# Softmax steps of two head groups merged, planner constants set anew, and ten more leading transposes, in an attention and two-MLP kernel on one core

## The chip, the cores and the metric

The kernel runs on one core of a Trainium2 chip. The metric is the device time of one execution in microseconds (us). The engines are TensorE (PE; its weight loads are listed apart as PEld), VectorE (DVE), ScalarE (ACT), GpSimd (POOL) and the queue SP, which issues the DMAs.

## The reference

Four batches of eight heads, 576 positions, head size 64. A softmax of `phi` over 32 memory slots pools the keys and values to 32 rows a head; each query attends to these 32 rows (a second softmax); the result, 2304 tokens by 512, goes through a leaky MLP (512 to 2048 to 512) and then through a bilinear one (512 to 1536, two branches multiplied, back to 512):

```python
a = exp(phi - max(phi));  a = a / (sum(a) + 1e-9)
k_m = einsum('bhsm,bhsd->bhmd', a, k);  v_m = einsum('bhsm,bhsd->bhmd', a, v)
s = (q @ k_m.T) / 8;  attn = exp(s - max(s));  attn = attn / (sum(attn) + 1e-9)
x = attn @ v_m                      # 2304 x 512 after the heads are joined
h = x @ w_in;  x = maximum(0.01 * h, h) @ w_out
out = ((x @ w_a) * (x @ w_b)) @ w_out2
```

The weights come as 64-bit floats and are cut to high and low single-precision parts on the chip; a product is the sum of three passes (high by high, low by high, high by low).

## The kernel before, in words

The attention is folded into the first MLP: the pooled values times `w_in` (`vw`, L704) are the weights that the softmax rows (`ahi`, `alo`) meet in `h` (L757). `h` goes through the leaky step on ACT to `g`; `g` times `w_out` is `y` (L796), summed over four chunks c of the 2048 columns into `acc`. From L1008 on the bilinear MLP runs in two halves s of the tokens with seven-product block schemes (`abx`, `abz`, `aby`, then `o` L1102 and `os` L1217).

The start of the program, for batch b and head group g (four heads each): `phi` is loaded (L520), its maximum (L540) and exponential (L541) taken, the result transposed on PE (`ta` L554, `tz` L557) and copied to `en`; `km` (L571) pools the keys and values from `kv` (L533) and a rest `kvr` (L536); `kvn` (L580) scales, `kvt` (L588) transposes, and copies make `kd` (pooled keys) and `vm` (pooled values). `sc` (L632) then makes the scores of one piece x of the positions (320 or 256 columns) for both row halves i, in two PSUM tiles. For each of these two, on its own: DVE transposes it to `sm` (L654), takes the maximum (L662), subtracts (L663); ACT exponentiates (L664); DVE sums, adds a small constant, takes the reciprocal (L667 to L669), multiplies (L672) and transposes back to `at` (L673); a copy gives `ahi` and a subtraction `alo` (L678). Four `win` tiles of chunk 0 (`raw_win`, `cv_win`, L454 to L478) must be converted before the first `vw`; four `wout` tiles (to L484) before the first `y`.

Nothing in the program fixes the order by hand. `Program.order` is a list planner: every operation has a cost per engine, a due time `late` and the tiles that it needs; at each moment an engine takes the ready operation with the earliest due time for which there is room. Due times are worked backwards (`urgency`): the due time of the earliest reader, less a latency (`LAT` between engines, `LAT_SAME` on one engine, `LAT_DMA` after a load), less the operation's own cost, less its `slack`. The targets at the end of this chain are the times of the main PE operations (`h`, `y`, `ab`, `o`), first guessed from `START`, then for five more rounds taken from the order just made; the shortest of the six orders is emitted. So a `slack` that is larger makes an operation, and all that leads to it, due earlier. `LEAD` is how many main operations may be taken ahead of the first one still open. `PE`, `DVE` and the others run what is emitted in that order, each engine in sequence. A tile takes a named room: `x` is three PSUM banks for `sc`, `vw`, `ta`, `tz`, `km` and `kvt`; `sm` has three rooms of its own; `slot` is the large pool of 28.

The 18 transposes at the very start (`warm`, L424) read only the identity matrix and write a tile that nobody reads.

Of the kernel before, what the change touches and what calls it, by code (L numbers as in the profile page):

```python
# [19 lines left out]
P = 128  # L20
# [14 lines left out]

NSLOT = 28
ROOMS = {
    "slot": [f"s{i}" for i in range(NSLOT)],  # L40
    "big": [f"g{i}" for i in range(8)],
    "five": [f"f{i}" for i in range(8)],
    "t": [f"t{i}" for i in range(5)],
    "sm": [f"m{i}" for i in range(3)],
    "kvn": ["kvn0"],
    "h": ["b0", "b1", "b2"],
    "y": ["b3", "b4"],
# [9 lines left out]
LEAD = 12
SLACK = {'phi0': 0.0, ('kv0', 0): 1.0, ('kv0', 1): 0.0, 'kvr0': 3.0, ('q0', 0): 0.0, ('q0', 1): 0.0, ('win0', 0): 5.37, ('win0', 1): 5.37, ('wout0', 0): 8.13, ('wout0', 1): 8.13, 'win': 4.9, 'wout': 4.64, 'wa': 23.6, 'wb': -0.15, 'wout2': 16.8, ('sc', 0, 0): 6.2, ('sc', 0, 1): 3.3, ('sc', 1, 0): 8.05, ('sc', 1, 1): 6.75, ('sc', 2, 0): 11.99, ('sc', 2, 1): 9.96, ('vw', 0, 0): 19.04, ('vw', 0, 1): 7.99, ('vw', 0, 2): 9.35, ('vw', 1, 0): -0.31, ('vw', 1, 1): 19.18, ('vw', 1, 2): 8.18}
START = 17.4
BIAS = 0.5  # L60
POOL_BIAS = 0.8
LAT, LAT_SAME, LAT_DMA = 0.4, 0.1, 1.0
OVER = {'PE': 0.0, 'ACT': 0.0, 'DVE': 0.0, 'POOL': 0.0, 'DMA': 0.0}
BLOCKED = 0.0
DMA_RATE, DMA_FIRST = 355e3, 0.0
# [40 lines left out]
class Program:  # L106
# [13 lines left out]
    def op(self, eng, cost, fn, r=(), w=(), tiles=(), pos=None, ahead=60.0, keep=0, slack=0.0, soon=False):  # L120
        o = Op()
        port = isinstance(eng, Port)
        o.costs = {e: (c - OVER[e]) * SPARE[e] for e, c in (eng if isinstance(eng, dict) else {eng: cost}).items()}
# [20 lines left out]
        self.ops.append(o)  # L144
        return o
# [188 lines left out]
def tile_mem_attention__leaky_mlp__bilinear_mlp(  # L334
# [283 lines left out]
    def sc_both(b, x):  # L618

        cols = piece(2 * b + x)  # L620
        n = cols.stop - cols.start
        qs = [("q", b, g) if b else ("q", b, g, x) for g in range(2)]
        scs = [("sc", b, i, x) for i in range(2)]
        for k in scs:
            tile_of(k, "x", [n])

        def s_sc(T):
            for g in range(2):
                for j in range(2):
# [8 lines left out]
        for i in range(2):  # L638
            sc_part(b, i, x)

    def sc_part(b, g, x):

        cols = piece(2 * b + x)
        n = cols.stop - cols.start
# [8 lines left out]
        tok = ("sm", b, g, x)
        op("DVE", c_dve(n), lambda T: nc.vector.transpose(T[sm].rearrange("p a m -> p (a m)"), T[sc]), r=[sc], w=[tok], tiles=[sc, sm])  # L654
        mx, sr = (stat((k, g, x, NM), NM) for k in ("mx", "sr"))
        kmx, ksr = ("mx", g, x, NM), ("sr", g, x, NM)
        by = two(n)
# [12 lines left out]

        op("DVE", c_dve(n) + 0.3, s_sum, r=[tok], w=[ksr], tiles=[sm])
        op(by, 0, lambda T, e: engines[e].tensor_tensor(T[sm], T[sm], wide(sr), op=ALU.mult), r=[ksr], w=[tok], tiles=[sm])  # L672
        op("DVE", c_dve(n), lambda T: nc.vector.transpose(T[at], T[sm].rearrange("p a m -> p (a m)")), r=[tok], w=[at], tiles=[sm, at])  # L673
        kh, kl = ("ahi", b, g, x), ("alo", b, g, x)
        op(copy_by(n), 0, lambda T, e: copy(e, T[ahi][:, g, cols], T[at]), r=[at], w=[kh], tiles=[at, ahi])
        op(
            two(n), 0,
            lambda T, e: engines[e].tensor_tensor(T[alo][:, g, cols], T[at], T[ahi][:, g, cols].bitcast(F32), op=ALU.subtract),  # L678
            r=[at, kh], w=[kl], tiles=[at, ahi, alo], slack=SLACK["sc", min(b, 2), x],
        )  # L680
# [678 lines left out]
```

## Time and profile before

| | us |
|---|---|
| median of 3 runs | 800.46 (800.13 to 802.74) |
| profiled execution, own time | 801.54 |
| its span, first to last instruction | 799.8 |
| PE busy | 775.5 (97%) |
| DVE busy | 615.9 (77%) |
| ACT busy | 372.6 (47%) |
| POOL busy | 119.9 (15%) |

The profile is that of one execution. "Busy" is the time in which an engine executed something; the granted clock is TensorE's, as a fraction of 2.4 GHz (0.50 is 1.2 GHz). The 40 slices of the page are 20 us each; a digit is the busy share in tenths.

### The profile page before, as it was taken

Reading aid. Unit: us, or ns where it says so; the run is one execution under the profiler, and the core shown is the slowest. Engines: PE = TensorE matmul, PEld = TensorE weight load, DVE = VectorE, ACT = ScalarE, POOL = GpSimd, SP = SyncE. Lnnn points to the kernel's source line nnn. Section 1 sums busy time; section 2 is a strip of 40 time slices with the busy share of each in tenths; the row PEclk is TensorE's granted clock in tenths of the full one; section 3 lists DMA queues with packets and bytes.
Section 4 is the critical chain, followed back from the end, with each engine's and each line's share of the span. In section 5 each row is a group of like instructions: output and inputs, shape, how many; then the busy total and the mean of one; then the engine's idle time right before and its main releaser. Section 6 shows DMA issues by size and latency. Waiting matters only on the chain. (4 is left out here: it accounts for less than half of the span.)

```text
span 799.8 us, 12802 instructions
## 1 busy us (share of the span) xinstructions
PE 775.5 (97%) x4754; PEld 661.9 (83%) x4754; DVE 615.9 (77%) x1179; ACT 372.6 (47%) x810; POOL 119.9 (15%) x176
## 2 busy tenths in 40 slices
PE   6689999999999999999999999999999999999998
PEld 4367788989898889899988888888888888888886
DVE  5797798689868986676756988998864666798855
ACT  4557676757444754444435635444321154232210
POOL 0132051014003500010000302131210100024100
PEclk6679999999999999999999999999999999999999
DMA  9974211367143722033878854666487988777402
GB/s 331 387 233 143 91 70 54 99 203 246 46 145 111 273 65 79 1 107 109 304 262 306 277 190 167 227 206 212 166 286 287 310 267 286 233 229 239 150 1 105
DMA packets 56558, 149.99 MB, mean 188 GB/s; under 512 B 7216, under 2 KB 22576, under 8 KB 56496
## 3 DMA queue, kind: packets, MB, share of 16 engines
q1 hardware_dynamic: 56496, 149.18, 54.8%
q8 instruction: 37, 0.61, 0.3%
q14 instruction: 25, 0.20, 0.1%
HBM read 103.55 MB, written 45.61 MB: 187 GB/s over the span
## 5 line engine op out<-in xcount | busy, mean ns | idle before, releaser
L796 PE MATMUL y<-g,wout 128*128 128x320 f32 (+1 forms) x1152 | 216.1, 340 | 1.0 <-DVE wout L484 0.8
L796 PEld LDWEIGHTS y<-g,wout 128*128 128x128 f32 x1152 | 187.5, 190 | 23.1 <-issue 6.3
L1008 PE MATMUL abx<-yb_T,wo 128*128 128x512 f32 x432 | 110.2, 390 | 0.0
L1102 PE MATMUL o<-p,wout 128*128 128x512 f32 x384 | 94.9, 390 | 0.0
L1008 PEld LDWEIGHTS abx<-yb_T,wo 128*128 128x128 f32 x432 | 80.2, 188 | 16.1 <-ACT t L1019 0.2
L1019 ACT COPY t<-abx 128x512 f32<-128x512 f32 x72 | 42.1, 585 | 101.9 <-PE abx L1008 101.7
L722 ACT ACTIVATE g<-h 128x320 fp32r<-128x320 f32 (+1 forms) x128 | 52.5, 411 | 70.8 <-PE h L757 66.9
L1102 PEld LDWEIGHTS o<-p,wout 128*128 128x128 f32 x384 | 72.0, 188 | 15.3 <-DVE osum L1115 0.4
L757 PE MATMUL h<-ahi,vwh 128*128 128x320 f32 (+1 forms) x256 | 78.5, 307 | 2.7 <-ACT ahi L405 1.8
L757 PE MATMUL h<-alo,vwh 128*128 128x320 f32 (+1 forms) x256 | 76.6, 299 | 1.3 <-POOL alo L388 1.0
L757 PE MATMUL h<-ahi,vwl 128*128 128x320 f32 (+1 forms) x256 | 76.3, 298 | 0.0
L811 DVE TENSOR_TENSOR acc<-y,acc 128x320 f32<-128x320 f32 (+1 forms) x72 | 40.1, 556 | 36.7 <-PE y L796 36.3
L773 DVE TENSOR_TENSOR g<-t,g 128x256 fp32r<-128x256 f32 (+1 forms) x112 | 52.5, 473 | 17.8 <-ACT t L722 17.0
L757 PEld LDWEIGHTS h<-ahi,vwh 128*128 128x128 f32 x256 | 48.9, 191 | 11.6 <-issue 4.5
L722 ACT ACTIVATE t<-h 128x320 f32<-128x320 f32 (+1 forms) x128 | 52.3, 409 | 0.2
L757 PEld LDWEIGHTS h<-alo,vwh 128*128 128x128 f32 x256 | 49.0, 191 | 2.6 <-POOL alo L388 1.6
L757 PEld LDWEIGHTS h<-ahi,vwl 128*128 128x128 f32 x256 | 49.0, 191 | 0.0
L1016 DVE TENSOR_TENSOR t<-abz,t 128x512 f32<-128x512 f32 x48 | 33.0, 687 | 20.0 <-ACT t L1019 10.9
L1115 DVE TENSOR_TENSOR oacc<-o,oacc 128x512 f32<-128x512 f32 x40 | 27.5, 688 | 14.8 <-PE o L1102 13.9
L405 ACT CAST p<-t 128x512 fp32r<-128x512 f32 x31 | 19.2, 620 | 39.9 <-DVE t L1040 26.1
L1008 PE MATMUL abx<-yb_B,wo 128*128 128x512 f32 x144 | 36.9, 392 | 0.0
L1008 PE MATMUL abz<-yb_B,wo 128*128 128x512 f32 x144 | 36.7, 390 | 0.0
(311 smaller groups left out, 1348.2 us busy)
## 6 DMA issues: line engine op xcount, KB each, us to landing
k_wo<-wo SPq DMA_DIRECT2D x32, 512.0 KB, 5.0
wo<-k_wo SPq DMA_DIRECT2D x32, 512.0 KB, 4.6
raw_wout<-in_w_out_dram SPq DMA_DIRECT2D x24, 512.0 KB, 5.6
raw_win<-in_w_in_dram SPq DMA_DIRECT2D x16, 512.0 KB, 5.5
kv<-in_kv_dram SPq DMA_DIRECT2D x16, 512.0 KB, 10.6
k_yb_T<-yb_T SPq DMA_DIRECT2D x8, 512.0 KB, 7.2
raw_wa<-in_w_a_dram SPq DMA_DIRECT2D x8, 512.0 KB, 4.1
raw_wb<-in_w_b_dram SPq DMA_DIRECT2D x8, 512.0 KB, 4.6
```

The lines of the kernel that those rows point to most:

```text
L405: nc.scalar.copy(dst, src)
L722: nc.scalar.activation(dst, src, AF.Prelu, alpha=0.01)
L757: nc.tensor.matmul(T[o], T[w[u]][:, k, fs], T[a[v]][:, k, cols], start=(k == 0 and i == 0), stop=(k == 1 and i == 2))
L773: lambda T, e: engines[e].tensor_tensor(T[g][:, i, 1, to], T[t], T[g][:, i, 0, to].bitcast(F32), op=ALU.subtract),
L796: nc.tensor.matmul(T[o], w[:, u, es], T[g][:, j, v, :], start=(f == 0 and p == 0), stop=(f == 3 and p == 2))
L811: "DVE", c_dve(m), lambda T: nc.vector.tensor_tensor(T[acc][:, i, :], T[o], T[acc][:, i, :], op=ALU.add),
L1008: nc.tensor.matmul(T[o], T[w][:, which, u, k * P:(k + 1) * P], T[ys[v]][:, k, :], start=first and k == 0 and x == 0, stop=k == 1 and x == ...
L1016: op("DVE", 0.69, lambda T: nc.vector.tensor_tensor(T[to], T[o], T[x], op=ALU.add), r=[o, x], w=[to], tiles=[o, x, to])
L1019: op("ACT", 0.59, lambda T: nc.scalar.copy(T[t], T[X]), r=[X], w=[t], tiles=[X, t])
L1102: nc.tensor.matmul(T[o], T[w][:, u, es], T[g][:, at, v, :], start=(x == 0 and k == 0), stop=(x == 1 and k == 2))
L1115: "DVE", c_dve(size), lambda T: nc.vector.tensor_tensor(T[acc][:, i, :], T[o], T[acc][:, i, :], op=ALU.add),
```

## The change

The two row halves of a piece get one `sm` tile, which now lies in a `slot` room (29 slots; the three `sm` rooms are gone). The first transposes and the last transposes, copies and `alo` stay one per half; maximum, subtraction, exponential, sum, reciprocal and multiplication are done once over both halves. `warm` issues 28 transposes. All planner constants are replaced. Core of the diff:

```diff
-NSLOT = 28
+NSLOT = 29
-    "sm": [f"m{i}" for i in range(3)],
+WARM = 28
-LEAD = 12
+LEAD = 9
-SLACK 'phi0': 0.0, ('kv0', 0): 1.0, ('kv0', 1): 0.0, 'kvr0': 3.0, ('q0', 0): 0.0, ('q0', 1): 0.0
+SLACK 'phi0': -5.09, ('kv0', 0): -2.57, ('kv0', 1): -8.21, 'kvr0': 3.72, ('q0', 0): -0.28, ('q0', 1): 1.39
-SLACK ('win0', 0): 5.37, ('win0', 1): 5.37, ('wout0', 0): 8.13, ('wout0', 1): 8.13, 'win': 4.9, 'wout': 4.64
+SLACK ('win0', 0): 3.41, ('win0', 1): 14.49, ('wout0', 0): 9.56, ('wout0', 1): 8.9, 'win': 2.74, 'wout': 8.15
-SLACK 'wa': 23.6, 'wb': -0.15, 'wout2': 16.8, ('sc', 0, 0): 6.2, ('sc', 0, 1): 3.3, ('sc', 1, 0): 8.05, ('sc', 1, 1): 6.75
+SLACK 'wa': 28.21, 'wb': -6.07, 'wout2': 14.85, ('sc', 0, 0): 10.3, ('sc', 0, 1): 2.94, ('sc', 1, 0): 7.58, ('sc', 1, 1): 4.46
-SLACK ('vw', 0, 0): 19.04, ('vw', 0, 1): 7.99, ('vw', 0, 2): 9.35, ('vw', 1, 0): -0.31
+SLACK ('vw', 0, 0): 17.13, ('vw', 0, 1): 8.31, ('vw', 0, 2): 6.08, ('vw', 1, 0): 5.69
-START = 17.4
+START = 15.74
-LAT, LAT_SAME, LAT_DMA = 0.4, 0.1, 1.0
+LAT, LAT_SAME, LAT_DMA = 0.4, 0.1, 1.75
-OVER = {'PE': 0.0, 'ACT': 0.0, ...}
+OVER = {'PE': 0.0, 'ACT': 0.043, ...}
-        for _ in range(18):
+        for _ in range(WARM):
...
-        tile_of(sm, "sm", [NM, M])
+        tile_of(sm, "slot", [2, NM, M])
+        for i in range(2):
+            op("DVE", c_dve(n), lambda T, i=i: nc.vector.transpose(T[sm][:, i]..., T[scs[i]]), r=[scs[i]], w=[toks[i]], ...)
-        op("DVE", c_dve(n), lambda T: nc.vector.tensor_reduce(mx, T[sm], axis=AX.X, op=ALU.max), r=[tok], w=[kmx], ...)
+        op("DVE", c_dve(2 * n), lambda T: nc.vector.tensor_reduce(mx, rows(T), axis=AX.X, op=ALU.max), r=toks, w=[kmx], ...)
-        op("ACT", c_act(n), lambda T: nc.scalar.activation(T[sm], T[sm], AF.Exp, ...), w=[tok], ...)
+        op("ACT", c_act(2 * n), lambda T: nc.scalar.activation(flat(T), flat(T), AF.Exp, ...), w=toks, ...)
...
+        for g in range(2):
+            op("DVE", c_dve(n), lambda T, g=g, at=at: nc.vector.transpose(T[at], T[sm][:, g]...), r=[toks[g]], w=[at], ...)
```

The planner's name for a load's slack carries the chunk: `('win0', x)` is the half x of `win` of chunk 0, `('kv0', g)` the `kv` of batch 0 and group g. `wa` and `wb` slacks are read by no operation: `weight` returns for these kinds ahead of the two operations that take them.

## Rows read from the trace of the kernel before

**Rows 1.** The page, part 1: busy us, share, instructions of PE; part 2: granted clock by slice.

```profile
PE 775.5 (97%) x4754; PEld 661.9 (83%) x4754; DVE 615.9 (77%) x1179; ACT 372.6 (47%) x810; POOL 119.9 (15%) x176
PEclk6679999999999999999999999999999999999999
```

**Rows 2.** Windows: stretch, its length, busy us by engine (instructions), granted clock, DMA share, GB/s.

```profile
0.00:75.00 75.00, 56.36 (x553) 40.33 (x553) 57.41 (x144) 40.81 (x108) 15.75 (x25) 0.77 0.83 291
75.00:796.00 721.00, 719.11 (x4203) 621.58 (x4201) 557.90 (x1036) 331.80 (x703) 104.16 (x151) 1.00 0.52 177
15.00:30.00 15.00, 11.83 (x126) 5.80 (x118) 8.28 (x27) 6.76 (x20) 0.00 (x0) 0.50 1.04 400
30.00:60.00 30.00, 22.84 (x208) 16.59 (x194) 28.31 (x65) 15.40 (x42) 10.01 (x12) 0.80 0.82 279
```

**Rows 3.** Timeline of all engines, 0 to 60 us: start, us, engine, line, operation.

```profile
2.72 1.04 SPq L454 DMA_DIRECT2D raw_win<-in_w_in_dram  x2
7.01 0.75 DVE L540 TENSOR_REDUCE kst<-phi 128x1 f32<-128x576 f32 x1
12.42 0.42 ACT L405 COPY en<-tz 64x128 f32<-64x128 f32 x2
21.93 0.46 DVE L407 COPY kd<-kvt 64x64 f32<-64x64 f32 x2 [1.25 <-ACT vm L405]
36.76 0.85 ACT L405 CAST ahi<-at 128x320 fp32r<-128x320 f32 x2 [3.03 <-DVE at L673]
48.52 2.63 DVE L484 TENSOR_TENSOR wout<-cv_wout,wout 128x512 fp32r<-128x512 f32 x2
```

**Rows 4.** Timeline of PE alone, 0 to 60 us.

```profile
1.36 3.71 PE L424 MATMUL warm<-ident 128*128 128x128 f32 x18 [1.36 <-POOL ident masks.py:199]
8.71 1.12 PE L554 MATMUL ta<-ident,phi 128*128 128x128 f32 x4 [3.65 <-ACT phi L541]
13.53 2.27 PE L571 MATMUL km<-kv,en 128*32 128x128 f32 x32 [2.17 <-DMA kv<-in_kv_dram]
24.34 1.10 PE L704 MATMUL vw<-cv_win,vm 64*32 64x256 f32 x14 [0.78 <-DVE vwl L714]
25.37 1.11 PE L554 MATMUL ta<-ident,phi 128*128 128x128 f32 x4
29.18 1.47 PE L632 MATMUL sc<-q,kd 64*32 64x320 f32 x16 [0.30 <-ACT en L405]
37.27 0.41 PE L757 MATMUL h<-ahi,vwh 128*128 128x320 f32 x1 [1.85 <-ACT ahi L405]
53.02 1.10 PE L704 MATMUL vw<-cv_win,vm 64*32 64x256 f32 x14 [0.86 <-DVE sm L654]
54.05 6.07 PE L796 MATMUL y<-g,wout 128*128 128x320 f32 x24
63.85 2.00 PE L796 MATMUL y<-g,wout 128*128 128x320 f32 x12
```

**Rows 5.** Windows again: around the clock's first fall and its second.

```profile
7.00:8.00 1.00, 0.00 (x0) 0.00 (x0) 1.00 (x3) 0.58 (x2) 0.00 (x0) 0.97 1.05 389
54.00:59.00 5.00, 5.00 (x25) 4.95 (x19) 4.83 (x12) 3.50 (x10) 1.47 (x2) 0.50 0.06 18
```

**Rows 6.** Groups by form, DVE and ACT: busy us, mean ns of one, idle before.

```profile
L662 DVE TENSOR_REDUCE mx<-sm 128x10 f32<-128x320 f32 x4 | 1.7, 458 | 0.0
L663 DVE TENSOR_TENSOR sm<-sm,mx 128x320 f32<-128x320 f32 x4 | 1.8, 483 | 0.0
L540 DVE TENSOR_REDUCE kst<-phi 128x1 f32<-128x576 f32 x8 | 5.8, 744 | 0.0
L842 DVE TENSOR_TENSOR yt_T<-acc,yt_T 128x640 f32<-128x640 f32 x4 | 3.3, 819 | 0.0
L669 DVE RECIPROCAL sr<-sr 128x10 f32<-128x10 f32 x4 | 0.9, 216 | 0.1
L664 ACT ACTIVATE sm<-sm 128x320 f32<-128x320 f32 x8 | 3.4, 470 | 3.0 <-DVE sm L663 3.0
```

More of the change, by code (lines that the diff above doesn't have):

```diff
@@ L55 @@
 TURN = 0.15
+WARM = 28
 SEVEN = 8
[L57 to L59 removed]
+LEAD = 9
+SLACK = {'phi0': -5.09, ('kv0', 0): -2.57, ('kv0', 1): -8.21, 'kvr0': 3.72, ('q0', 0): -0.28, ('q0', 1): 1.39, ('win0', 0): 3.41, ('win0', 1): 14.49, ('wout0', 0): 9.56, ('wout0', 1): 8.9, 'win': 2.74, 'wout': 8.15, 'wa': 28.21, 'wb': -6.07, 'wout2': 14.85, ('sc', 0, 0): 10.3, ('sc', 0, 1): 2.94, ('sc', 1, 0): 7.58, ('sc', 1, 1): 4.46, ('sc', 2, 0): 12.17, ('sc', 2, 1): 10.7, ('vw', 0, 0): 17.13, ('vw', 0, 1): 8.31, ('vw', 0, 2): 6.08, ('vw', 1, 0): 5.69, ('vw', 1, 1): 20.3, ('vw', 1, 2): 8.21}
+START = 15.74
 BIAS = 0.5
[L61 to L63 removed]
+POOL_BIAS = 0.82
+LAT, LAT_SAME, LAT_DMA = 0.4, 0.1, 1.75
+OVER = {'PE': 0.0, 'ACT': 0.043, 'DVE': 0.0, 'POOL': 0.0, 'DMA': 0.0}
 BLOCKED = 0.0
[L65 removed]
+DMA_RATE = 355000.0
 SPARE = {'PE': 1.0, 'ACT': 1.03, 'DVE': 1.03, 'POOL': 1.03, 'DMA': 1.2}
@@ L422, in warm @@
     def warm(T):
-        for _ in range(18):
+        for _ in range(WARM):
             nc.tensor.transpose(T["warm",], ident, ident)
-    op("PE", 5.0, warm, tiles=[("warm",)], ahead=1e12)
+    op("PE", 0.28 * WARM, warm, tiles=[("warm",)], ahead=1e12)
     src_of = {
@@ L637, in sc_both @@
         op("PE", 4 * n / 2.4e3 + TURN, s_sc, r=[*qs, *(("kd", b % 2, g) for g in range(2))], w=scs, tiles=[*qs, *scs])
[L638 to L644, printed above, removed]
         NM = n // 32
-        sc, sm, at = ("sc", b, g, x), ("sm", b, g, x), ("at", b, g, x)
-        tile_of(sm, "sm", [NM, M])
-        tile_of(at, "t", [n])
-        ahi, alo = ("ahi", b), ("alo", b)
+        sm, ahi, alo = ("sm", b, x), ("ahi", b), ("alo", b)
@@ L651, in sc_part, with flat @@
+        tile_of(sm, "slot", [2, NM, M])
         tile_of(ahi, "big", [2, S], F32R)
         tile_of(alo, "big", [2, S], F32R)
[L653 to L657, printed above, removed]
+        toks = [(sm, i) for i in range(2)]
+        def flat(T):
+            return T[sm].rearrange("p i a m -> p (i a m)")
@@ L659, in wide, with rows @@
+        def rows(T):
+            return T[sm].rearrange("p i a m -> p (i a) m")
+        for i in range(2):
+            op(
+                "DVE", c_dve(n), lambda T, i=i: nc.vector.transpose(T[sm][:, i].rearrange("p a m -> p (a m)"), T[scs[i]]),
+                r=[scs[i]], w=[toks[i]], tiles=[scs[i], sm],
+            )
+        mx, sr = (stat((k, x, NM), 2 * NM) for k in ("mx", "sr"))
+        kmx, ksr = ("mx", x, NM), ("sr", x, NM)
         def wide(t):
-            return t.unsqueeze(2).to_broadcast([P, NM, M])
@@ L662, in sc_part @@
-        op("DVE", c_dve(n), lambda T: nc.vector.tensor_reduce(mx, T[sm], axis=AX.X, op=ALU.max), r=[tok], w=[kmx], tiles=[sm])
-        op(by, 0, lambda T, e: engines[e].tensor_tensor(T[sm], T[sm], wide(mx), op=ALU.subtract), r=[kmx], w=[tok], tiles=[sm])
-        op("ACT", c_act(n), lambda T: nc.scalar.activation(T[sm], T[sm], AF.Exp, scale=1.0 / float(D) ** 0.5), w=[tok], tiles=[sm])
+            return t.unsqueeze(2).to_broadcast([P, 2 * NM, M])
+        op("DVE", c_dve(2 * n), lambda T: nc.vector.tensor_reduce(mx, rows(T), axis=AX.X, op=ALU.max), r=toks, w=[kmx], tiles=[sm])
@@ L666, in s_sum @@
+        op(two(2 * n), 0, lambda T, e: engines[e].tensor_tensor(rows(T), rows(T), wide(mx), op=ALU.subtract), r=[kmx], w=toks, tiles=[sm])
+        op("ACT", c_act(2 * n), lambda T: nc.scalar.activation(flat(T), flat(T), AF.Exp, scale=1.0 / float(D) ** 0.5), w=toks, tiles=[sm])
         def s_sum(T):
-            nc.vector.tensor_reduce(sr, T[sm], axis=AX.X, op=ALU.add)
+            nc.vector.tensor_reduce(sr, rows(T), axis=AX.X, op=ALU.add)
             nc.vector.tensor_scalar_add(sr, sr, EPS)
@@ L669, in s_sum @@
             nc.vector.reciprocal(sr, sr)
[L671 to L680, printed above, removed]
+        op("DVE", c_dve(2 * n) + 0.3, s_sum, r=toks, w=[ksr], tiles=[sm])
+        op(two(2 * n), 0, lambda T, e: engines[e].tensor_tensor(rows(T), rows(T), wide(sr), op=ALU.mult), r=[ksr], w=toks, tiles=[sm])
+        for g in range(2):
+            at = ("at", b, g, x)
+            tile_of(at, "t", [n])
+            op("DVE", c_dve(n), lambda T, g=g, at=at: nc.vector.transpose(T[at], T[sm][:, g].rearrange("p a m -> p (a m)")), r=[toks[g]], w=[at], tiles=[sm, at])
+            kh, kl = ("ahi", b, g, x), ("alo", b, g, x)
+            op(copy_by(n), 0, lambda T, e, g=g, at=at: copy(e, T[ahi][:, g, cols], T[at]), r=[at], w=[kh], tiles=[at, ahi])
+            op(
+                two(n), 0,
+                lambda T, e, g=g, at=at: engines[e].tensor_tensor(T[alo][:, g, cols], T[at], T[ahi][:, g, cols].bitcast(F32), op=ALU.subtract),
+                r=[at, kh], w=[kl], tiles=[at, ahi, alo], slack=SLACK["sc", min(b, 2), x],
+            )
```

## The prediction

> **What bounds the kernel now.** The page comes first: PE is busy 97% of the span, and its clock is low only in the first three slices of 20 us [rows 1]. Cutting the span in two tells where time can still be had: from 75 to 796 us PE is busy 719.1 of 721 us at full clock, whereas the first 75 us hold 18.6 us without PE work and a mean clock of 0.77 [rows 2]. So behind 75 us PE itself is the bound and 1.9 us is all that a better order could give there, while a worse one can take any amount; the gain has to come from the start. That leaves two questions for the timelines: what keeps the first `h` until 37.27 us, and what keeps PE from running through between there and 60 us [rows 4].
>
> For the first, the chain runs phi, `ta`, `km`, `kvt`, `kd`, `sc`, softmax, `ahi`, `h`. `kd` is finished at 22.39 us [rows 3], yet `sc` starts at 29.18: PE does the second half of `vw` (24.34) and the transposes of batch 1 (25.37) ahead of it [rows 4]. This is order, not data. For the second, DVE is busy 28.3 of 30 us between 30 and 60 us, where between 15 and 30 it had only 8.3 of 15 [rows 2]: a DVE-bound stretch behind a half idle one.
>
> **The change, part by part.**
>
> *`sc` moves up.* Due times can be worked out from the code; T is the target of the first `h`. Before, back from T over `alo`, `ahi`, transpose, multiplication, sum, exponential, subtraction, maximum, transpose and `sc`, with latencies of 0.1 or 0.4 and slack 6.2, `sc` is due at T-14.4. The two halves of `vw` are due at T-21.7 and T-19.9 (slack 19.04, the second for an `h` 1.76 later). So both `vw` go first, as the timeline shows. After, slack 10.3 and the doubled costs put `sc` at T-20.1, and slack 17.13 puts `vw` at T-19.7 and T-17.9. `sc` is now the most urgent, and I take it to start behind one half of `vw`, at 24.3 instead of 29.18: 4.9 us. Both ends: 6.8 us if it starts when `kd` is there (22.4), 0 if PSUM rooms or the greedy choice leave it where it is.
>
> *The loads change places.* The same arithmetic before gives `win` half 0 at T-33.8, phi T-32.1, `win` half 1 T-32.0, `kvr` T-30.8, `kv` T-29.7, and SP issues in just that order, `win` half 1 third at 2.72 us [rows 3], which is why I trust it. After: `win` half 1 T-39.8 (slack 14.49), `kvr` T-30.8, `win` half 0 T-30.6, phi T-26.2 (slack -5.09), `kv` of group 0 T-25.3, `q` T-22.7, `kv` of group 1 T-19.7. So phi comes behind 1.05 MB of `win` and 0.26 MB of `kvr` that it preceded; at the 389 GB/s of that time [rows 5] that is 3.4 us. `kv` of group 0 has the same bytes ahead of it as before. `en` was complete at 12.84 us and `km` waited for `kv` until 13.53 [rows 3, 4], so 0.7 us of the delay is covered and `km` comes 2.7 us later. Ends: 0 (ACT and DVE free of the interleaved conversions catch up) and 3.4. I take 2.7. It falls on the same chain as the gain of `sc`: the first `h` comes 4.9 - 2.7 = 2.2 us earlier.
>
> *The merged softmax.* Per piece of 320, the four operations over 320 columns that become one of 640 are maximum, subtraction, sum and multiplication: eight of 0.46 to 0.48 us become four. A DVE operation with two inputs takes 0.819 us at 640 columns; a maximum over 576 columns takes 0.744, and by its slope one over 640 some 0.82 [rows 6]. That saves 2x0.458-0.82 = 0.10 twice and 2x0.483-0.819 = 0.15 twice, plus one reciprocal (0.22 [rows 6]) and one addition that I put at the same: 0.94 us of DVE. Three pieces lie ahead of 60 us, so 2.8 us of DVE work go; with DVE 94% busy from 30 to 60, PE gets about 2.5 of them. Ends: 2.8, and 0 if what held PE there were PSUM rooms (the `vw` at 53.02 waited for the DVE transpose of `sm`). The later five pieces save 4.7 us of DVE under a full PE: nothing.
> The merged chain itself is not shorter. Before, `sc` ended at 30.65 and `ahi` began at 36.76, 6.1 us. After: two transposes 0.92, maximum 0.82, subtraction 0.82, exponential some 0.8 (between 0.47, its time at 320 [rows 6], and twice that), sum and its two small ones 1.25, multiplication 0.82, transpose 0.46, two hops between engines 0.2: 6.1. What is lost is that ACT worked on one half while DVE did the other; DVE has an idle 0.9 us during the exponential, into which a `wout` conversion fits.
>
> *Ten more transposes.* 18 take 3.71 us, so 28 end at 1.36 + 5.8 = 7.1 us instead of 5.07. PE was idle until 8.71 anyway [rows 4], and with phi later until some 12.1; nothing waits behind them. What they could give is clock. It stayed at 1.00 until close to 8 us, 2.9 us after the last transpose, and was 0.50 until 31 [rows 2, 5]. The same 2.9 us from 7.1 on end at 10, ahead of `ta` at 12.1: nothing. If phi is not delayed, `ta` and `tz` run at full clock until the wait for `kv`, worth 1 us at most.
> The Trainium skill (TensorE: Matmul & The Clock Gate, Part 4: PE-mode transpose) says that transposes don't count as PE activity for the clock; if so even that 1 us is gone. The trace can't decide it: the clock was full from the first instruction and fell after the transposes had ended.
>
> *The rest.* The slacks of `wa` and `wb` are read by nobody, so these edits are nothing. A slot more, fewer rooms for `sm`, `LEAD` 9, `win` 2.74, `wout` 8.15, `wout2` 14.85 reorder work under a full PE: 0, covered by 163 us of idle DVE from 75 us on [rows 2]; if the cover fails, each late weight costs its conversion, about 0.7 us.
>
> *Sum.* 2.2 + 2.5 = 4.7 us off 801.54, the profiled execution's own time (span 799.8 and 1.7 around it): 796.8. The median of the runs is 1.1 below that execution, so 795.8 for a median.
>
> **The rivals.**
>
> *Full clock (A).* From 54 to 59 us PE works at 0.50 [rows 5] because it had paused at 52 to 53: 24 `y` matmuls take 6.07 us where 12 at full clock take 2.00 [rows 4], so 2.1 us. If the denser order closes this pause, and `sc` starts at 22.4, the sum is 4.7 + 2.1 + 1.9 = 8.7: 791.8. For it: merged tiles free the PSUM rooms of `sc` in two consecutive transposes. Against: DVE remains full, so the pause is likely to move rather than to close.
>
> *Absorbed (B).* The first `h` comes earlier, but `y` waits for `wout`, whose low parts end on DVE at 51.15 us [rows 3], and DVE does the same work up to there less 1.9 us (two pieces), while the phi delay costs DVE the same idle time in front: 800 within 2. For: DVE at 94%. Against: 6.7 us of idle DVE from 15 to 30, which an earlier `sc` fills.
>
> *Slower (C).* phi is late and `sc` doesn't move. The place is `en` at 12.84 against `kv` at 13.53: once `en` comes later than `kv`, each us is one on the whole chain. Then 2.7 us later for `h`, nothing back from DVE, and 1.5 us of stalls in the order made anew behind 75 us, where only loss is possible: 801.54 + 4.2 - 1.1 = 804.6. For: the due times; PE has no slack later to win it back. Against: the same due times move `sc`.
>
> *The change does not do what it says:* the planner emits the best of six rounds by its own length; if its costs place the softmax on DVE in the same gaps, order and time stay as they are. This ends with B at 800.
>
> **How the numbers follow.** The forecast, 793.5 to 798, has 0.45; A 0.16; B with the unchanged order 0.17; C 0.22. The range leaves out the far ends of A (below 789.5) and C (above 803.5): 789.5 to 803.5; the forecast's own range is 793.5 to 798. A measurement of this kernel tells 0.3%, 2.4 us, from no change. Faster by more than that, below 798.1: forecast and A, 0.61; within: B, 0.17; slower, above 802.9: C, 0.22.
>
> **What would show it.** `sc` at 24 to 27 us and the first `h` near 35 show the first step right; `ta` near 12 and `km` near 16 the second. DVE busy between 30 and 60 with about 1 us less per softmax piece, the maximum over 640 columns at 0.82, show the third. The clock at 0.50 from 10 us on shows the transposes idle; a clock of 1.00 at 13 us would make me wrong there. Waits of PE behind 75 us above 3 us in all would show the loss of C. The prediction is wrong if the first `h` does not move earlier and the time falls all the same, or if the time from 75 us on changes by more than the start.

## The result, and the profile after

The changed kernel takes 791.78 us (median of four runs, 790.38 to 792.52) against 800.30 us for the kernel before on the same chip (four runs, 799.77 to 802.74): ratio 0.9886, 95% interval 0.9861 to 0.9911. The forecast was 795.8: right in direction and inside the range, but the gain is 8.5 us where 4.7 were forecast. The profiled execution took 792.19 us, against 801.54 before.

The page of the changed kernel, parts 1 and 2, as in [rows 1]:

```profile
PE 769.7 (97%) x4764; PEld 660.3 (84%) x4764; DVE 604.3 (76%) x1120; ACT 376.4 (48%) x811; POOL 131.6 (17%) x190
PEclk8699999999999999999999999999999999999999
```

PE still has 97%; it is busy 5.8 us less in all, and the low digits of the clock are two instead of three. The same windows as [rows 2]:

```profile
0.00:75.00 75.00, 59.60 (x615) 45.38 (x616) 56.59 (x132) 47.48 (x123) 13.85 (x24) 0.86 0.84 291
75.00:786.00 711.00, 709.63 (x4150) 614.85 (x4149) 547.02 (x988) 328.92 (x688) 117.71 (x166) 1.00 0.53 179
15.00:30.00 15.00, 10.00 (x145) 5.08 (x143) 9.79 (x22) 9.86 (x26) 4.51 (x7) 0.84 1.03 407
30.00:60.00 30.00, 26.97 (x287) 21.03 (x273) 26.72 (x66) 18.46 (x52) 6.51 (x10) 0.82 0.94 321
```

Behind 75 us there is 1.4 us without PE work now, 1.9 before: nothing came from there. In the first 75 us PE does 59.6 us of work at a mean clock of 0.86, where it did 56.4 at 0.77. DVE is busier from 15 to 30 us (9.8 against 8.3) and less busy from 30 to 60 (26.7 against 28.3). PE's timeline, to be laid beside [rows 4]:

```profile
1.36 5.71 PE L424 MATMUL warm<-ident 128*128 128x128 f32 x28 [1.36 <-POOL ident masks.py:199]
13.08 1.12 PE L554 MATMUL ta<-ident,phi 128*128 128x128 f32 x4 [6.01 <-ACT phi L541]
15.41 1.65 PE L571 MATMUL km<-kv,en 128*32 128x128 f32 x32
...
21.03 1.78 PE L632 MATMUL sc<-q,kd 64*32 64x320 f32 x16
...
34.25 0.65 PE L571 MATMUL km<-kvr,en 64*32 64x128 f32 x8 [1.83 <-DMA kvr<-in_kv_rest_dram]
34.83 1.94 PE L571 MATMUL km<-kv,en 128*32 128x128 f32 x32
...
37.28 0.63 PE L760 MATMUL h<-ahi,vwh 128*128 128x320 f32 x1
...
46.28 2.03 PE L799 MATMUL y<-g,wout 128*128 128x320 f32 x12
48.23 0.66 PE L707 MATMUL vw<-cv_win,vm 64*32 64x256 f32 x16
48.83 5.55 PE L799 MATMUL y<-g,wout 128*128 128x320 f32 x36
```

`sc` starts 8.2 us earlier than before (21.03 against 29.18) and yet the first `h` starts at the same time (37.28 against 37.27). The gain comes behind it: 36 `y` follow each other in 5.55 us, where before 12 `y`, a pause, and 24 `y` at half clock stood.

To see where, the matmuls of `h` and `y` (and of the later stages) are numbered from the first `h`, number 0; number 24 is the first `y`, number 36 the thirteenth. Their starts, changed kernel minus kernel before: number 0, 0.0; 24, -1.8; 36, -5.2; 60, -7.5; 144, -9.1 (73.01 against 82.12 us); 600, -9.0; the last one, -9.4. So 5.2 us come between the first `h` and the thirteenth `y`, 2.3 in the next 24 matmuls, 1.6 from there to number 144, and 0.3 in the remaining 713 us.

In the kernel before, PE is idle for 3.9 us between the first `h` and the thirteenth `y`, and in the changed kernel for 1.2. The later waits of the kernel before are for DVE: `y` waits for low parts of the first `wout` weights (L484), and the `vw` at 53.02, right ahead of the thirteenth `y` [rows 4], for a transpose of `sm` that DVE does behind the last of these parts. This last part ended at 51.15 us before [rows 3] and ends at 45.88 now, 5.3 us earlier; in the changed kernel PE waits for nothing between 44.75 us and the thirteenth `y`. The transpose of the kernel before, and the last low part of the changed one:

```profile
52.57 0.40 DVE L654 STREAM_TRANSPOSE sm<-sc 128x256 f32<-128x256 f32 x1
```

```profile
45.20 0.68 DVE L484 TENSOR_TENSOR wout<-cv_wout,wout 128x512 fp32r<-128x512 f32 x1
```

Windows from 15 us up to the end of the last low part, the kernel before and then the changed one:

```profile
15.00:51.15 36.15, 26.73 (x277) 15.90 (x269) 28.11 (x67) 17.64 (x48) 8.55 (x10) 0.72 1.03 376
```

```profile
15.00:45.88 30.88, 22.85 (x282) 14.24 (x283) 23.38 (x53) 18.32 (x49) 11.02 (x16) 0.75 1.04 374
```

DVE's idle time is nearly the same (8.0 and 7.5 us). It is the busy time that fell, from 28.1 to 23.4 us, by 4.7. The groups of DVE from the start up to those two ends, each instruction counted whole, with the mean ns of one behind the comma:

```profile
L475 DVE SCALAR_TENSOR_TENSOR cv_wout<-raw_wout,cv_wout 128x512 int32<-128x512 int32 x4 | 3.8, 1017 | 0.0
L484 DVE TENSOR_TENSOR wout<-cv_wout,wout 128x512 fp32r<-128x512 f32 x3 | 3.3, 1131 | 0.0
L475 DVE SCALAR_TENSOR_TENSOR cv_win<-raw_win,cv_win 128x512 int32<-128x512 int32 x4 | 2.7, 687 | 0.0
L663 DVE TENSOR_TENSOR sm<-sm,mx 128x320 f32<-128x320 f32 (+1 forms) x4 | 2.4, 638 | 0.0
```

```profile
L475 DVE SCALAR_TENSOR_TENSOR cv_wout<-raw_wout,cv_wout 128x512 int32<-128x512 int32 x4 | 2.6, 670 | 0.0
L484 DVE TENSOR_TENSOR wout<-cv_wout,wout 128x512 fp32r<-128x512 f32 x3 | 2.3, 776 | 0.3 <-ACT wout L405 0.3
L663 DVE TENSOR_TENSOR sm<-sm,mx 128x640 f32<-128x640 f32 (+1 forms) x2 | 1.5, 749 | 0.0
```

The four joins L475 on `cv_wout` took 1017 ns each before, though the same operation on `cv_win` took 687: 670 now. The three L484 took 1131 and take 776. These are not other operations, they ran beside other work. The kernel before's joins and its second pair of subtractions in DVE's timeline, and POOL's timeline around them:

```profile
37.34 3.84 DVE L475 SCALAR_TENSOR_TENSOR cv_wout<-raw_wout,cv_wout 128x512 int32<-128x512 int32 x4
47.09 1.51 DVE L663 TENSOR_TENSOR sm<-sm,mx 128x256 f32<-128x256 f32 x2
```

```profile
37.30 2.13 POOL L388 TENSOR_TENSOR alo<-at,ahi 128x320 fp32r<-128x320 f32 x2 [35.99 <-ACT ahi L405]
46.45 2.88 POOL L388 TENSOR_TENSOR g<-t,g 128x320 fp32r<-128x320 f32 x3
49.59 1.02 POOL L388 TENSOR_TENSOR g<-t,g 128x320 fp32r<-128x320 f32 x1 [0.26 <-ACT t L722]
```

The long joins begin at 37.34, the long L484 at 48.52 [rows 3]: both run beside POOL's subtractions for `alo` and `g`. In the changed kernel POOL does its clamps at 24.98 and 28.57 us, `alo` is on DVE, and POOL is idle from 33.7 to 40.1. Of the fall, then, the joins give 1.2 us and L484 1.0. The softmax lines (L654 to L673 before, L653 to L676 after) give 1.6, of which some 0.75 is again L663, at 1.51 us for two of 256 columns where two beside no POOL work take 0.75 (`pool_cut`, below), and 0.4 a sum of the second piece that had just begun at 51.08; some 0.45 is left for the merge. Copies of `en`, `kd` and `wout` that went to ACT give 1.6, clamps that went to POOL 0.7; `alo` costs 0.9 more, other lines 0.5 more. That is 4.7.

### The profile page after: what moved, and what is told of

It reads as the page before. It is cut to its first block, busy times and chain, and to the rows that moved or that the text cites. A ratio compares the mean times of both kernels' runs of the same rounds, so it can differ in the third digit from the quotient of the medians.

```text
span 790.4 us, 12768 instructions
## 1 busy us (share of the span) xinstructions
PE 769.7 (97%) x4764; PEld 660.3 (84%) x4764; DVE 604.3 (76%) x1120; ACT 376.4 (48%) x811; POOL 131.6 (17%) x190
## 4 chain that ended last, share of the span: by engine, by line
PE 93%; DMA 5%; DVE 1%; SPq 1%; issue 0%; ACT 0%; DVEq 0%; ACTq 0%
PE y L799 26%; PE abx L1011 16%; PE h L760 14%; PE o L1105 13%; PE abz L1011 8%; PE os L1220 5%; PE aby L1011 4%; PE b L1065 2%; PE vw L707 2%; PE a L1065 2%; DMA kvr<-in_kv_rest_dram 2%; PE km L571 2%; DMA k_wo<-wo 1%; DMA phi<-in_phiT_dram 1%; PE sc L632 1%; DMA raw_wout<-in_w_out_dram 1%
## 5 line engine op out<-in xcount | busy, mean ns | idle before, releaser
L799 PEld LDWEIGHTS y<-g,wout 128*128 128x128 f32 x1152 | 185.0, 188 | 18.1 <-issue 3.0
L776 DVE TENSOR_TENSOR g<-t,g 128x320 fp32r<-128x320 f32 (+1 forms) x110 | 51.6, 477 | 16.2 <-ACT t L725 15.8
```

The source lines that it names most:

```text
L776: lambda T, e: engines[e].tensor_tensor(T[g][:, i, 1, to], T[t], T[g][:, i, 0, to].bitcast(F32), op=ALU.subtract),
L799: nc.tensor.matmul(T[o], w[:, u, es], T[g][:, j, v, :], start=(f == 0 and p == 0), stop=(f == 3 and p == 2))
```

## The experiments

Three questions: which part of the change carries the gain; whether DVE's work, as the prediction had it, is what PE gets back; and what the clock and the idle transposes are worth. Ratios are to the kernel before, run on the same chip. This table has the chain of every kernel whose order matters below (us; "wout" is the end of the last low part on DVE):

| kernel | first `h` | wout | 13th `y` | number 144 | ratio (95%) |
|---|---|---|---|---|---|
| before | 37.27 | 51.15 | 54.05 | 82.12 | 1 |
| changed | 37.28 | 45.88 | 48.83 | 73.01 | 0.9886 (0.9861 to 0.9911) |
| merge_only | 40.66 | 51.95 | 56.89 | 81.07 | 0.9982 (0.9965 to 0.9999) |
| consts_only | 35.95 | 42.73 | 49.36 | 73.58 | 0.9890 (0.9852 to 0.9928) |
| sc_up | 32.88 | 47.90 | 50.66 | 75.10 | 0.9946 (0.9925 to 0.9967) |
| sc_and_loads | 38.53 | 49.19 | 51.94 | 76.40 | 0.9975 (0.9955 to 0.9994) |
| old_loads | 31.92 | 45.42 | 50.74 | 73.47 | 0.9951 (0.9932 to 0.9970) |
| old_sc | 45.40 | 51.01 | 57.84 | 81.60 | 0.9957 (0.9936 to 0.9978) |
| less_dve | 36.79 | 49.77 | 52.44 | 78.52 | 0.9969 (0.9954 to 0.9985) |
| less_more | 36.44 | 47.42 | 50.10 | 75.91 | 0.9938 (0.9919 to 0.9956) |
| pool_cut | 37.81 | 48.24 | 50.70 | 77.56 | 0.9965 (0.9950 to 0.9981) |
| dve_mid | 37.43 | 46.57 | 49.16 | 73.35 | 0.9901 (0.9870 to 0.9932) |
| dve_second | 35.19 | 48.72 | 50.98 | 75.16 | 0.9906 (0.9886 to 0.9927) |

The starts are those of one profiled execution each. That of the kernel before took 801.54 us, 0.3 to 1.3 us above the medians beside which the ratios stand; those of `old_sc` and `old_loads` lie 3.4 and 2.7 us above their own medians, that of `dve_mid` 2.1 below. Number 144 is a mark for the whole start only where the same other work lies ahead of it: from there to number 600 PE does 83.4 us of work in the changed kernel, but 87.0 in `old_loads` and 84.6 in `consts_only`.

### Which part carries it

**merge_only**: the kernel before with the merged softmax, its rooms, and nothing else.

```diff
-NSLOT = 28
+NSLOT = 29
...
-        for i in range(2):
-            sc_part(b, i, x)
+        # the merged steps of the changed kernel
```

> The kernel before with the merged softmax alone (and the 29th slot that it needs); constants and 18 transposes as before. Theory (the new order of the start carries the gain: DVE and ACT convert the weights of the first y earlier, so PE does not pause at 51 to 54 us and keeps its clock): sc stays behind both halves of vw near 29 us, the pause near 52 us stays, some 1 to 3 us faster than before, 797 to 799. Rival (the DVE work that the merge saves carries it): 8 to 9 us faster, near 791.5, with no half clock behind 52 us.

Measured 800.32 against 801.25 us, ratio 0.9982. The planner's new order puts the first `h` at 40.66 and holds an `sc` for a PSUM room that the softmax frees late:

```profile
52.48 1.31 PE L631 MATMUL sc<-q,kd 64*32 64x320 f32 x14 [3.55 <-DVE sm L652]
53.73 6.84 PE L798 MATMUL y<-g,wout 128*128 128x320 f32 x36
```

So the merge with the old constants is worth 0.2%, less than the 1 to 3 us expected: fewer DVE instructions, in an order that waits.

**consts_only**: the changed kernel with the softmax of before, one half at a time.

```diff
-NSLOT = 29
+NSLOT = 28
+    "sm": [f"m{i}" for i in range(3)],
...
+        for i in range(2):
+            sc_part(b, i, x)
```

> The changed kernel with the softmax of before, one operation per half (28 slots and three rooms for sm); new constants and 28 transposes. Theory: sc moves up to 21 to 24 us as in the changed kernel, the pause near 52 us is closed, 5 to 8 us faster than before, 792 to 795. Rival (merge): at most 2 us faster, 798 or more.

794.39 us, 0.9890: with its interval it can't be told from the changed kernel. The constants carry nearly the whole gain, by the order that they make (the 28 transposes, which this kernel has too, give nothing: `warm18`, below).

**sc_up**: the kernel before with two constants of after. **sc_and_loads**: those, the load slacks and the DMA latency. **old_loads** and **old_sc**: the changed kernel with the load slacks, or the two `sc`/`vw` slacks, of before. The first two lines below are `sc_up` (and `old_sc`, the other way round), the last two are in `sc_and_loads` too (and `old_loads`, the other way round).

```diff
-SLACK ('sc', 0, 0): 6.2, ('vw', 0, 0): 19.04
+SLACK ('sc', 0, 0): 10.3, ('vw', 0, 0): 17.13
...
-SLACK 'phi0': 0.0, ('kv0', 0): 1.0, ..., ('win0', 0): 5.37, ('win0', 1): 5.37
+SLACK 'phi0': -5.09, ('kv0', 0): -2.57, ..., ('win0', 0): 3.41, ('win0', 1): 14.49
```

> The kernel before with two constants of the changed one: slack of the first sc 10.3 (was 6.2) and of the first vw 17.13 (was 19.04). All else as before. Theory (the early sc lets DVE do the softmax of the first piece in its idle time before 30 us, so that wout is ready earlier and the pauses near 50 us go): half or more of the gain, 793 to 797. Rival (order of the loads, phi late and win early, carries it): within 2 us of before, 799 to 802.

> The kernel before with the slacks of the first sc and vw, of the first loads (phi0, kv0, kvr0, q0, win0) and the latency of a load (1.75) from the changed kernel; softmax, transposes and all other constants as before. Theory (these two groups, each worth about 4 us by itself, put the first softmax and the weight conversions into DVE's idle time): 791.5 to 794.5, the whole gain within 2 us. Rival (the rest of the constants, or chance in the planner's other choices, holds half of it): 795 to 799.

> The changed kernel with the load slacks of before (phi0, kv0, kvr0, q0, win0). Theory: phi comes 3 to 4 us earlier, ta near 9 to 10 us, sc near 19 to 20; the first h stays near 36 to 37 because it stands behind the pooling of batch 1, which waits for its loads; total within 2 us of the changed kernel, 790 to 794. Rival (load order carries it): back to 797 to 801.

> The changed kernel with slack 6.2 for the first sc and 19.04 for the first vw, as before. Theory: sc goes behind both halves of vw again (26 to 30 us), the first softmax ends later, 3 to 6 us slower than the changed kernel: 794 to 798. If the merged softmax and the loads carry it alone: 791 to 793.

`sc_up` takes 796.54 us: two numbers give half of the gain. `sc_and_loads`, with more of the new constants, was expected to give the whole gain and gives no more (798.48; the two intervals overlap): the groups don't add up, each constant is worth what the order around it makes of it. `old_loads` (796.89), expected within 2 us of the changed kernel, is some 5 us slower, although it has the earliest `h` of all, 31.92 us: an early `h` by itself buys nothing. `old_sc` (797.49) has the first `h` at 45.40, since `km` of batch 1 waits 5.5 us for the PSUM room that the softmax still holds; the earlier `sc` is needed.

### Whether DVE's work is what PE gets

**dve_mid** and **dve_second**: the changed kernel, order unchanged, a merged maximum taken N times: five for the first piece in `dve_mid`, six for the second in `dve_second`. **dve_idle**: six additions of 128 columns on DVE at 15.4 us, in an idle stretch.

```diff
-lambda T: nc.vector.tensor_reduce(mx, rows(T), axis=AX.X, op=ALU.max)
+lambda T: [nc.vector.tensor_reduce(mx, rows(T), axis=AX.X, op=ALU.max) for _ in range(N)]
```

> The changed kernel, same order on every engine; the maximum of the first merged softmax is taken five times instead of once, at 24.5 us: 3.3 us more of DVE work. Theory (DVE sets the pace from the first sc to the first y): the last wout conversion and the first y come 2.5 to 3.5 us later and so does the end, 793.5 to 795.5. Rival (loads and PE's own order set the pace, DVE has room): first y under 1 us later, 791 to 792.5.

> The changed kernel, same order on every engine, with six additions over 128 columns (1.4 us or so) at 15.4 us on DVE, where it was idle for 2 us. Theory: nothing changes, 790.5 to 792.5; the place of DVE work counts, not its amount. If DVE work counts wherever it lies: 1 to 1.5 us slower.

> The changed kernel, its order unchanged, with the merged maximum of the second piece (batch 0, 512 columns, at 44.61 us) taken six times: 3.3 us more DVE right ahead of the last wout part and of the vw at 48.2. If DVE bounds this stretch in the changed kernel too: the y and vw from 48 us on come 3 us later, with a pause that lowers the clock again, matmul 144 at 76 to 79, total 795 to 797. If DVE has room there, as it had at 24 us: matmul 144 within 1 us of 73.0, total within 1.5 us of the changed kernel.

3.4 us more of DVE from 24.6 us on move the last low part by 0.7 us and the thirteenth `y` by 0.3: up to there DVE has room in the changed kernel, and the theory that it sets the pace from the first softmax on falls. The total, 792.71, says less: the traced execution took 790.56 us, the other three 792.26 to 794.59, and its interval holds both no loss and a loss of 3 us. `dve_idle`: 791.01 (0.9884, 0.9859 to 0.9909), nothing, as expected. Some 3.6 us more, 20 us later, are another thing:

```profile
48.77 0.42 PE L799 MATMUL y<-g,wout 128*128 128x320 f32 x1 [1.39 <-DVE wout L484]
49.12 0.62 PE L707 MATMUL vw<-cv_win,vm 64*32 64x256 f32 x2
50.39 0.66 PE L707 MATMUL vw<-cv_win,vm 64*32 64x256 f32 x14 [0.66 <-DVE sm L653]
50.98 5.54 PE L799 MATMUL y<-g,wout 128*128 128x320 f32 x36
```

The last of the first twelve `y` waits 1.4 us for the low part of `wout`, `vw` 0.7 for the softmax; everything from there to number 600 comes 2.15 us later, and the total is 794.28. The expectation had 3 us, a fall of the clock and number 144 at 76 to 79; the clock did not fall (36 `y` in 5.54 us).

**less_dve** and **less_more**: the kernel before, order unchanged, with DVE work taken out of the first three softmax pieces: `less_dve` from one half, `less_more` from both (the multiplication is cut like the subtraction shown) and from the joins of the first `wout` (the last three lines). **less_fill** is `less_more` with the idle transposes of `before_fill` (below).

```diff
+        cut = 1 if (b, x) in ((0, 0), (0, 1), (1, 0)) and g in HALVES else NM
-engines[e].tensor_tensor(T[sm], T[sm], wide(mx), op=ALU.subtract)
+engines[e].tensor_tensor(part(T), part(T), wide(mx)[:, :cut], op=ALU.subtract)
...
-            nc.vector.scalar_tensor_tensor(a, words(T, I32, 1), -0x40000000, a, ...)
+            n = 32 if kind == "wout" and c == 0 else 512
+            nc.vector.scalar_tensor_tensor(a[:, :n], words(T, I32, 1)[:, :n], -0x40000000, a[:, :n], ...)
```

> The kernel before, its order unchanged. In the first three softmax pieces the subtraction and the multiplication of one half work on one slot block of 32 columns instead of all (the rest is left out, and the exponential of that half gets a scale that keeps it finite). That takes some 0.8 us of DVE from each piece, 2.3 in all, about what the merged steps save. The prediction's step (what DVE is spared between 30 and 60 us, PE gets): the first y some 1 to 1.5 us earlier than 48.10, matmul 144 at 79.6 to 80 instead of 82.12, total about 798. Rival (the order and the pause hold PE; saved DVE time falls into gaps): matmul 144 within 0.7 us of 82.1, total within 1 us of before.

> The same order, with the subtraction and the multiplication of both halves cut to 32 columns in the first three pieces, and the joining step of the first wout weights (L475) cut from 512 to 32 columns: their remainder is left out. Some 4.5 us and some 2.5 to 4 us less DVE ahead of 55 us. If the work of DVE is what separates the two kernels up to 75 us: first y by 45 to 46 us, the pause at 50 to 54 closed, 24 y of 54.05 in 4 us or less, matmul 144 at 73 to 75, total 791 to 793. If the order of PE and the weights' arrival hold it: matmul 144 at 79 or later, total above 797.

> The same cuts as in the run with both halves and the joining step cut, and four idle transposes in each of the two waits around the first y matmuls. If DVE's work opens the pause and the clock makes the rest of it: matmul 144 no more than 0.5 us apart from the run without the transposes, since no pause is left. If a pause is left and costs clock: 1.5 to 2.3 us earlier than that run.

`less_dve`: the last low part comes 1.4 us earlier, the thirteenth `y` 1.6, and the 24 `y` behind it take 3.79 us instead of 6.07, because the pause has become short:

```profile
51.85 0.66 PE L708 MATMUL vw<-cv_win,vm 64*32 64x256 f32 x14 [0.21 <-DVE sm L654]
52.44 3.79 PE L800 MATMUL y<-g,wout 128*128 128x320 f32 x24
```

798.42 against 800.99 us. So this step of the prediction holds in the old order: DVE time is PE time there, and closing the pause adds the clock. `less_more` goes on (number 144 at 75.91; 796.63), short of the 73 to 75 and the 791 to 793 expected: DVE's busy time from 15 us to the end of the last low part is 23.6 us there, nearly that of the changed kernel (23.4), but this gives 6.2 of the 9.1 us at number 144 and 4.4 of the 8.5 us in all. So DVE's work is some two thirds of the gain at the start; what else in the new order gives the rest was not separated. `less_fill` has the same start (76.11), as expected where no pause is left, and 795.40 (0.9924, 0.9907 to 0.9942).

**pool_cut**: the kernel before, order and DVE's instructions unchanged; POOL's early subtractions become memsets (for `alo`, shown, and likewise for `g` of the first piece and the low part of the first `wout`).

```diff
-lambda T, e: engines[e].tensor_tensor(T[alo][:, g, cols], T[at], T[ahi]..., op=ALU.subtract),
+lambda T, e: engines[e].zero(T[alo][:, g, cols]) if e == "POOL" and b == x == 0 else
+    engines[e].tensor_tensor(T[alo][:, g, cols], T[at], T[ahi]..., op=ALU.subtract),
...
+        def zero(self, dst):
+            nc.gpsimd.memset(dst.bitcast(F32), 0.0)
```

> The kernel before, its order and DVE's instructions unchanged. POOL's subtractions ahead of the first y (low parts of ahi at 37.3 us, of one wout part at 43.9, of g at 46.5) are replaced by a short POOL memset of the same tile, which reads no SBUF; the low parts so set to zero are left out of the result. In the kernel before, DVE's two-input operations beside these took longer than elsewhere: the four joins L475 3.84 us instead of four times 0.68, the two subtractions L663 1.51, the last two L484 2.63 instead of 1.36. Theory (DVE waits while POOL reads): these fall to 2.7, 1.0 and 1.4, in all 2.9 us; the last wout part ends at some 48.2 instead of 51.15, the 36th y comes at 51 instead of 54.05, the 24 y behind it run at full clock, matmul 144 comes 5 to 6 us earlier, total 795 to 796. Rival (these operations are slow for another reason, or PE is held by its own order): the three groups keep their times, matmul 144 within 1 us of 82.1, total within 1 us of before.

```profile
37.88 2.49 DVE L478 SCALAR_TENSOR_TENSOR cv_wout<-raw_wout,cv_wout 128x512 int32<-128x512 int32 x4
46.28 0.75 DVE L668 TENSOR_TENSOR sm<-sm,mx 128x256 f32<-128x256 f32 x2
46.95 1.29 DVE L489 TENSOR_TENSOR wout<-cv_wout,wout 128x512 fp32r<-128x512 f32 x2
```

Joins 2.49 us instead of 3.84, L663 (L668 here) 0.75 instead of 1.51, the two L484 (L489) 1.29 instead of 2.63: about 3.4 us of DVE's busy time were waiting for POOL. The last low part ends 2.9 us earlier, the thirteenth `y` (the "36th" of the expectation, by its number) comes 3.4 us earlier, number 144 4.6. The total is 797.48 against 800.24, less than expected: number 144 fell short by half a us, the profile that it is held against is 1.3 us above its median, and from number 144 on PE waits 0.5 us more than in the kernel before (0.7 us at 437 and 0.9 at 644). The cut takes away POOL's own time as well: in `less_dve` two of the first twelve `y` wait 0.56 us, until 50.54, for POOL's `g`, and in `pool_cut` none does. So DVE's wait of 3.4 us is shown, but the gain in time is that of both.

### The clock and the transposes

**warm18**, **warm58**: the changed kernel, planned alike, with 18 or 58 leading transposes emitted. **fill**: with 7, 7 and 10 more in PE's waits of batch 1 (`ta`, `tz`, `km`). **before_fill**: the kernel before with four in the wait around its first `y` (shown) and four in that of `vw`.

```diff
-        for _ in range(WARM):
+        for _ in range(18):
...
+        def filler(T, n):
+            for _ in range(n):
+                nc.tensor.transpose(T["warm",], ident, ident)
...
+                    if hold and f == 1 and p == 0:
+                        filler(T, 4)
```

> The changed kernel with 18 leading transposes instead of 28, planned as 28, so that the order of all else is the same. Theory: the clock falls near 8 us instead of 9.9, PE is idle until 13.1 in both, no change within 1 us: 791 to 793. Rival (the ten transposes are what raises the clock again at 16 us, because the chip starts to look at another moment): the clock comes up later than 16 us and the time is 1 to 3 us longer.

> The changed kernel with 58 leading transposes, planned as 28, which fill PE up to the first real work at 13.1 us. Theory: the clock stays at 1.00 through 13 us, the ta, tz and first km run at full clock, but the km waits for loads and sc for kd: sc up to 1 us earlier; 0 to 1.5 us faster than the changed kernel. If transposes do not count as activity the clock falls near 10 us all the same and nothing changes.

> The changed kernel, its order unchanged on every engine, with 7 idle transposes in the ta and 7 in the tz of batch 1 and 10 in its first km, where PE waited 1.6, 1.5 and 1.8 us between 25 and 34 us. If the half clock from 27 to 40 us comes of these pauses, the clock stays up, km and the first twelve h run at full clock and it is 1.5 to 3 us faster than the changed kernel: 789 to 790.5. If the waits for loads set the pace there, first h at 36 to 37 and under 1 us.

> The kernel before, its order unchanged on every engine, with four idle transposes inside the first y (its wait for wout near 49 us) and four inside the vw that waits near 52 us, so that PE is not idle there. If the clock that fell at 52.6 us is a price of these pauses alone, the clock stays at 1.00 behind 52 us, the next 24 y matmuls take 3.6 instead of 6.07 us and the kernel is 2 to 2.5 us faster than before (798 to 799). If the waits themselves (for wout and for PSUM) are what the changed kernel saved, this gives nothing more; if the clock falls by other rules, no change.

`warm18` 790.62 us (0.9847, 0.9815 to 0.9878), `warm58` 790.48 (0.9853, 0.9822 to 0.9884), `fill` 790.24 (0.9859, 0.9837 to 0.9881): neither ten transposes fewer nor 30 more, nor the filled waits, can be told from the changed kernel. In `fill` the weight loads of the first `h` take 188 ns, where they take 330 in the changed kernel, so the clock was up there, and the first `h` and `y` come 1.1 and 1.2 us earlier; 0.4 us of this is left at number 144. `before_fill` shows the clock alone:

```profile
54.08 3.79 PE L804 MATMUL y<-g,wout 128*128 128x320 f32 x24
```

24 `y` in 3.79 us instead of 6.07 [rows 4], number 60 is 2.3 us earlier, and the total is 801.41 against 800.71 (1.0005, 0.9985 to 1.0025): 2 us at this place, of which 1.0 is given back up to number 144 and the rest by waits at 560 and 648 us. None of these versions beats the changed kernel by more than can be measured.

## Why the prediction was right or wrong

**Loads.** Right. SP issues `win` four times, `kvr`, phi, `kv`, `q`, `kv`, the order worked out but for `kvr`, whose due time is 0.2 us from that of `win` half 0; `ta` starts at 13.08 us (about 12.1 forecast) and `km` 1.9 us later than before (2.7 forecast).

**`sc` moves up.** The mechanism was right, the size beyond my bound: 8.2 us, where I took 4.9 and at most 6.8, for PE did the later `km` and `kvt` at full clock (0.84 on average from 15 to 30 us, 0.50 before), and `kd` was there in time although `km` began late.

**"The first `h` comes 4.9 - 2.7 = 2.2 us earlier."** Wrong: 0.0. `ahi` and `alo` were ready at 34.83 us (the line below), so its own inputs would have allowed it; but `km` of batch 1 stands ahead of it on PE, waited until 34.25 for `kvr` and ran to 37.3. I moved one chain and did not ask what would stand before its end in the new order. By the sign that I had set ("wrong if the first `h` does not move earlier and the time falls all the same") the prediction fails here.

```profile
33.95 0.88 DVE L681 TENSOR_TENSOR alo<-at,ahi 128x320 fp32r<-128x320 f32 x2
```

**"With DVE 94% busy from 30 to 60, PE gets about 2.5 of them."** This is the term that was mis-sized: 9.1 us came there, 5.2 of them up to the thirteenth `y`. Its mechanism held in part: `less_dve` and `dve_second` show that DVE's time is PE's time there, `less_more` that it is some two thirds of the 9.1. What was wrong is the count of DVE's work. The rows said that DVE's time up to the last `wout` part is the bound, and I counted from them only what the merge removes; rival B even says "DVE does the same work up to there less 1.9 us". It did 4.7 us less. The merge gave some 0.45 of that, and so less than I had counted. Some 2.9 was DVE's wait for POOL, which stood in my rows unread: [rows 3] has two L484 at 2.63 us, twice the usual time. The rest was work moved to ACT and POOL and a sum of the second piece that no longer falls ahead of this end. That the forecast came within 4 us is luck: 2.2 us for an earlier `h` that did not come, and a merge taken too large, stood in for the wait and the moved work, which it did not have.

**The pause and the clock.** Against rival A the prediction says that "the pause is likely to move rather than to close". It closed, and that gave 2.3 us at numbers 36 to 60 (A: 2.1); how much of it counts at the end is open, since `before_fill` lost the same 2.3 us again. A's 791.8 is the measured time nearly to the digit, but not by its route, since its 2.2 and 1.9 us for an earlier `h` came to nothing. The remaining 1.6 us up to number 144 are the end of PE's waits there: PE was busy 20.82 of 22.16 us before and 20.56 of 20.56 after.

**The merged chain and the transposes.** The times of the merged operations were right: maximum 0.81, subtraction 0.82, exponential 0.74 us at 640 columns (0.82, 0.82 and about 0.8 worked out). What they spare was not. Two maxima of 320 columns in the kernel before, and the one of the changed kernel:

```profile
31.59 0.84 DVE L662 TENSOR_REDUCE mx<-sm 128x10 f32<-128x320 f32 x2
```

```profile
24.54 0.81 DVE L662 TENSOR_REDUCE mx<-sm 128x20 f32<-128x640 f32 x1
```

I took twice the mean of one, 0.92 us, but the second starts (31.95) before the first has ended (32.03). Over the first piece the softmax keeps DVE busy for 5.5 us before and 5.1 now: 0.4 us a piece, where I had 0.94. The granted clock fell at 9.8 us (10 forecast), and the transposes gave nothing. But "the clock was full from the first instruction" was wrong; see below.

**Behind 75 us.** Right: 0.3 us. C's mechanism had no place, since `sc` moved.

**Open.** `os` at 640 to 650 us waits for ACT or DVE, which wait for the store of converted weights: 1.2 us in the changed kernel's profile, none in `warm18`, `fill` and `dve_mid` with the same order, 2.6 in `sc_and_loads`. What delays the store was not tried.

## What to carry to other kernels

Before work on a saturated engine is counted, compare each group's mean with the same operation elsewhere in the trace: a group at 1.5 times its usual time may hold a wait that the busy share hides, as here, and an order that separates the two engines takes it away. Find the one instruction that releases the stretch (here the last `wout` part on DVE: in the two kernels, `sc_up`, `sc_and_loads`, `less_dve`, `less_more`, `pool_cut`, `dve_mid` and `dve_second` the thirteenth `y` comes 2.3 to 3.0 us behind it; in `merge_only`, `consts_only`, `old_loads` and `old_sc` it comes 4.9 to 6.8 us behind, and other work stands before it) and count everything ahead of it, not only what the change removes. Where a list planner makes the order, a constant is worth what the whole order makes of it: two constants alone gave half the gain, and more of them gave no more.

## What the runs showed of the hardware

DVE operations with two inputs wait for POOL operations that read SBUF: the join L475 takes 687 ns alone and up to 1366 beside POOL's subtractions; in `less_more` a join of 32 columns takes 178 ns alone and up to 904 beside them, so the time is a wait and not a slower rate. POOL waits as well: in the changed kernel one clamp of 128 columns, begun at 26.77 us just behind DVE's L663, takes 1278 ns where those ahead of it take 634, and L663 takes its usual 0.82 us. The Trainium skill (SBUF — State Buffer, SBUF: two separate sides) has this rule: a DVE operation with two SBUF inputs and a GpSimd operation that reads SBUF use one pair of ports, which the one that starts first holds for its whole instruction. The trace agrees, by this clamp and this L663, and so does `pool_cut`: without POOL's reads 3.4 us of DVE time are gone.

By its weight loads TensorE starts at the half clock. Those of `ta` in the kernel before take 226 ns at 25.4 us, at a granted clock of 0.50, and 140 at 61.3 us, at 1.00. Those of the leading transposes of the changed kernel show both times (duration in ns: least, median and most):

```profile
L424 PEld LDWEIGHTS warm<-ident x28: 140/230/230, 1.4 to 6.7; 128*128 128x128 f32 x28
```

They take 230 ns at first and 140 from 6.4 us on (from 4.5 us in the kernel before; in `warm18` all 18, to 5.0 us, take 230), so the clock rose while PE did nothing but transposes, which decides what the prediction left open. The granted clock shows 1.00 from the first instruction on all the same. In `before_fill` it shows 1.00 for the whole span (mean 1.000), while the weight loads of `h` take 330 ns at 40 us and 190 at 45: where the clock matters, the duration of a weight load is the better witness.
